# Three loads instead of five for the down weights of a decode step, with thirty-one unread products

## The chip, the cores and the metric

The kernel runs on one core of one Trainium2 chip. The metric is device time in microseconds (us), the median of repeated executions. One execution of each kernel was also taken with the hardware profiler; its span is some 2 us shorter than the time.

## The reference, cut to what matters

One token, model width 1024, passes an attention block with a large key and value cache and then a gated feed-forward layer of inner width 3584. The last step is what this study is about:

```python
h2 = h + (gelu(n @ w_gate) * (n @ w_up)) @ w_down     # n = layernorm(h); w_down is 3584 x 1024, bf16, 7.3 MB
```

All weights and caches, 173 MB, are read once.

## The kernel before

All loads go through one on-chip ring of 5 units of 16384 columns; SyncE issues them in program order and waits where a load overwrites data that is still to be read. The 28 "rows" of the down weights (128 x 1024 values each, 256 KB) come in five loads of falling size. Behind each load stand its products: per row four products of 128x256, one for each group of 32 output columns of the array, accumulating in the tile `f_ps`. Between them stand *unread products*: `keep_busy` multiplies data that is already there by an identity into a tile that nobody reads. They only give TensorE something to do while it would wait.

```python
def load(src, off=0):                       # next free place of the ring, one DMA
    ...
    nc.sync.dma_start(out=tv.rearrange("p (n w) -> p n w", w=w), in_=src)

# ... gate weights: one load; up weights: two loads of four rows, products into wu_ps, then
# transposes wu_t, the gate's product act_bf and its zero-padded form actz ...

wd_v = B_w_down.rearrange("(p c) n -> p c n", p=P)     # a load of n rows: n*2 KB in one run per partition
sizes = [14, 7, 4, 2, 1]
actz = padded(rows, act_bf[:], FC, "actz")
w_ps = row_bank("w_ps")

def keep_busy(n, src):
    for _ in range(n):
        mm(w_ps[:], ident_bf[:], src, True, True)      # 128x512, never read

keep_busy(8, wu[:, 0, 0:512])
busy = [3, 2, 1, 0, 0]
c0 = 0
for sz, nb in zip(sizes, busy):
    at[0] = 0
    wv = load(wd_v[:, c0:c0 + sz, :], c0 * D)
    for cc in range(sz):
        c = c0 + cc
        out_mm(actz[:, c, :], lambda g: wv[:, cc, g * OW:(g + 1) * OW], False, c + 1 == FC)   # 4 products
    c0 += sz
    keep_busy(nb, wv[:, 0, 0:512])
nc.vector.tensor_copy(out=o_fin[0:97, :], in_=f_ps[0:97, :])
nc.sync.dma_start(out=out[0, 0].rearrange("(g n) -> g n", n=OW), in_=o_fin[0:97:32, :])
```

## Time and profile before

| | before |
|---|---|
| time, median of 3 | 408.4 us (408.33 to 408.57) |
| span of the profiled run | 406.9 us |
| HBM reads | 173.02 MB at 425 GB/s |
| from the last up weights' landing to the last down weights' landing | 17.05 us |
| from the last landing to the end of the last product | 0.36 us |

The page of the profile, cut to four lines. The second and third have one digit for each fortieth of the span, in tenths: the clock granted to TensorE, and the busy share of the 16 DMA engines.

```profile
span 406.9 us, 2667 instructions
...
PEclk9986899987989999899996998999989899886889
DMA  9999999999999999999999999999999999999995
...
HBM read 173.02 MB, written 0.00 MB: 425 GB/s over the span
```

DMA is busy from the first slice to the last. Nothing that TensorE does counts unless it comes after the last landing or delays an issue. The end of the chain of waits (start, duration, what) says the same of the tail:

```profile
373.51 29.95 DMA ring<-in_B_w_down_dram
...
403.51 0.32 PE f_ps L145 x4
...
403.85 0.42 DVE o_fin L558
```

The timeline of TensorE's matmuls in the tail (start, duration, engine, line, operation, tiles, form, count; in brackets the idle time before and who ended it):

```profile
386.46 0.62 PE L145 MATMUL wu_ps<-ring,hnz 128*32 128x512 bf16 x4 [6.48 <-DMA ring<-in_B_w_up_dram]
...
391.47 1.89 PE L145 MATMUL w_ps<-ring,ident_bf 128*128 128x512 bf16 x8
395.00 1.71 PE L145 MATMUL f_ps<-ring,actz 128*32 128x256 bf16 x56 [1.63 <-DMA ring<-in_B_w_down_dram]
396.64 0.82 PE L145 MATMUL w_ps<-ring,ident_bf 128*128 128x512 bf16 x3
399.24 0.95 PE L145 MATMUL f_ps<-ring,actz 128*32 128x256 bf16 x28 [1.78 <-DMA ring<-in_B_w_down_dram]
400.12 0.61 PE L145 MATMUL w_ps<-ring,ident_bf 128*128 128x512 bf16 x2
401.67 0.62 PE L145 MATMUL f_ps<-ring,actz 128*32 128x256 bf16 x16 [0.94 <-DMA ring<-in_B_w_down_dram]
402.22 0.39 PE L145 MATMUL w_ps<-ring,ident_bf 128*128 128x512 bf16 x1
402.89 0.40 PE L145 MATMUL f_ps<-ring,actz 128*32 128x256 bf16 x8 [0.28 <-DMA ring<-in_B_w_down_dram]
403.51 0.29 PE L145 MATMUL f_ps<-ring,actz 128*32 128x256 bf16 x4 [0.21 <-DMA ring<-in_B_w_down_dram]
```

Each batch of `f_ps` products waits for its load: the starts at 395.00, 399.24, 401.67, 402.89 and 403.51 follow the landings by 0.04 to 0.05 us. TensorE has time to spare in every gap, and only the last four products lie behind the last landing.

### The profile page before, as it was taken

What the parts mean: (1) busy time and instruction counts of PE and PEld (TensorE: products, weight loads), DVE (VectorE), ACT (ScalarE), POOL (GpSimd) and SP (SyncE); (2) the same over time, 40 slices, a digit from 0 to 9 for tenths busy, and PEclk for the clock granted to TensorE, in tenths of its full rate; (3) what the DMA queues carried; (4) which work ended last, traced back from release to release, by engine and by line L of the source; (5) the groups of instructions that cost most, each with busy time, mean ns of one, the idle gap of its engine ahead of it and who ended that gap; (6) DMA issues with size and microseconds to landing.
All of it is one profiled execution on the core that took longest, in us unless ns stands there. A gap on an engine that the chain in (4) does not pass through costs nothing.

```text
span 406.9 us, 2667 instructions
## 1 busy us (share of the span) xinstructions
PE 293.1 (72%) x1495; PEld 60.8 (15%) x743; DVE 202.7 (50%) x185; ACT 44.7 (11%) x67; POOL 7.4 (2%) x17
## 2 busy tenths in 40 slices
PE   1346777769977699597776979976597969636283
PEld 0011111111111112111110111111111101212031
DVE  1118899955978359147971880879433000220110
ACT  1010000022000040100000420000041000100000
POOL 2000000000000000000000000000100000100000
PEclk9986899987989999899996998999989899886889
DMA  9999999999999999999999999999999999999995
GB/s 367 457 412 448 427 419 461 413 444 424 415 464 419 409 499 414 393 438 425 490 414 403 448 425 435 417 457 432 445 438 432 433 399 435 445 436 414 437 419 222
DMA packets 5213, 173.19 MB, mean 426 GB/s; under 512 B 585, under 2 KB 593, under 8 KB 849
## 3 DMA queue, kind: packets, MB, share of 16 engines
q1 hardware_dynamic: 5192, 173.02, 98.7%
q8 instruction: 9, 0.15, 0.1%
q14 instruction: 4, 0.02, 0.0%
q10 hardware_dynamic: 8, 0.00, 0.0%
HBM read 173.02 MB, written 0.00 MB: 425 GB/s over the span
## 4 chain that ended last, share of the span: by engine, by line
DMA 53%; PE 31%; DVE 12%; ACT 2%; issue 0%; SPq 0%; ACTq 0%
DMA ring<-in_A_v_cache_dram 31%; PE acc_ps L147 11%; DVE ring L281 9%; PE qk_ps L145 7%; DMA ring<-in_A_k_cache_dram 7%; DMA ring<-in_B_w_down_dram 7%; DMA ring<-in_B_w_gate_dram 7%; PE qk_ps L147 7%; PE acc_ps L145 4%; DVE mx L302 2%; ACT sc L301 2%; PE wg_ps L145 0%; PE wg_ps L147 0%; DVE pT L330 0%; ACT pe_r L327 0%
## 5 line engine op out<-in xcount | busy, mean ns | idle before, releaser
L281 DVE STREAM_TRANSPOSE ring<-ring 128x2048 uint32<-128x2048 uint32 x64 | 142.7, 2280 | 33.6 <-DMA ring<-in_A_k_cache_dram 33.5
L145 PE MATMUL qk_ps<-ring,wsel 128*128 128x512 bf16 x256 | 100.8, 394 | 35.8 <-DVE mx L302 23.6
L147 PE MATMUL acc_ps<-ring,pT 128*128 128x512 bf16 x384 | 114.1, 409 | 0.0
L147 PE MATMUL qk_ps<-ring,wsel 128*128 128x512 bf16 x256 | 100.6, 393 | 0.0
L145 PE MATMUL acc_ps<-ring,pT 128*128 128x512 bf16 x128 | 52.7, 412 | 20.4 <-DMA ring<-in_A_v_cache_dram 17.6
L145 PEld LDWEIGHTS <-wsel 128*128 128x128 bf16 x256 | 25.4, 99 | 135.1 <-issue 134.4
L301 ACT COPY sc<-qk_ps 128x1024 f32<-128x1024 f32 x16 | 16.2, 1011 | 176.8 <-PE qk_ps L147 176.7
L302 DVE TENSOR_REDUCE mx<-qk_ps 128x1 f32<-128x1024 f32 x16 | 19.6, 1222 | 26.0 <-ACT sc L301 26.0
L145 PEld LDWEIGHTS <-pT 128*128 128x128 bf16 x128 | 13.3, 104 | 119.1 <-issue 113.2
L357 DVE COPY acc_sb<-acc_ps 32x512 f32<-32x512 f32 x8 | 5.4, 672 | 36.6 <-PE acc_ps L147 36.6
L327 ACT ACTIVATE pe_r<-sc,nbias 128x1024 bf16<-128x1024 f32 x16 | 18.2, 1140 | 39.2 <-DVE nbias L322 38.5
L330 DVE STREAM_TRANSPOSE pT<-pe_r 128x1024 bf16<-128x1024 bf16 x16 | 19.0, 1226 | 6.2 <-ACT pe_r L327 6.2
L359 ACT COPY acc_sb<-acc_ps 32x512 f32<-32x512 f32 x8 | 4.6, 577 | 65.0 <-DVE acc_sb L357 65.0
L145 PE MATMUL q_ps<-ring,xnz 128*32 128x512 bf16 x32 | 5.2, 623 | 7.9 <-DMA ring<-in_A_wq_dram 7.9
L145 PE MATMUL wu_ps<-ring,hnz 128*32 128x512 bf16 x32 | 4.7, 503 | 7.8 <-DMA ring<-in_B_w_up_dram 7.8
L145 PE MATMUL wg_ps<-ring,hnz 128*32 128x512 bf16 x32 | 4.6, 517 | 7.7 <-DMA ring<-in_B_w_gate_dram 7.7
L145 PE MATMUL ln_tot<-ln_s,ones_f 128*128 128x1 f32 x8 | 1.9, 312 | 10.8 <-DVE ln_s L199 9.0
L315 DVE TENSOR_REDUCE gm<-mxT_ps 1x8 f32<-1x128 f32 x4 | 1.1, 279 | 16.1 <-PE mxT_ps L156 16.1
L145 PE MATMUL o_ps<-sel,acc_sb 128*128 128x8 f32 x32 | 4.2, 257 | 6.5 <-DVE rl L371 5.7
L145 PE MATMUL f_ps<-ring,actz 128*32 128x256 bf16 x112 | 4.0, 274 | 4.8 <-DMA ring<-in_B_w_down_dram 4.8
L237 DVE COPY q_ev<-q_ps 128x512 f32<-128x512 f32 x1 | 0.7, 692 | 13.3 <-PE q_ps L147 13.3
L237 DVE COPY wg_ev<-wg_ps 128x512 f32<-128x512 f32 x1 | 0.7, 691 | 11.6 <-PE wg_ps L145 11.6
(103 smaller groups left out, 89.2 us busy)
## 6 DMA issues: line engine op xcount, KB each, us to landing
ring<-in_A_k_cache_dram SPq DMA_DIRECT2D x16, 4096.0 KB, 33.9
ring<-in_A_wq_dram SPq DMA_DIRECT2D x2, 4096.0 KB, 16.5
ring<-in_A_wo_dram SPq DMA_DIRECT2D x2, 4096.0 KB, 30.8
ring<-in_B_w_gate_dram SPq DMA_DIRECT2D x1, 7168.0 KB
ring<-in_B_w_up_dram SPq DMA_DIRECT2D x2, 3584.0 KB, 30.5
ring<-in_B_w_down_dram SPq DMA_DIRECT2D x1, 3584.0 KB, 37.1
ring<-in_B_w_down_dram SPq DMA_DIRECT2D x1, 1792.0 KB
ring<-in_B_w_down_dram SPq DMA_DIRECT2D x1, 1024.0 KB, 29.3
```

The source lines that it names most:

```text
L145: return pe(t.matmul(out, lhsT=lhsT, rhs=rhs, start=start, stop=stop, tile_position=tile_position, skip_group_check=skip_group_check))
L147: op = t.add_instruction(mybir.InstMatmult(name=nc.get_next_instruction_name(), engine=t.engine, start_tensor_calc=start, stop_tensor_calc ...
L237: nc.vector.tensor_copy(out=dst, in_=src)
L281: dv(nc.vector.transpose(out=kt[:, c * w:(c + 1) * w], in_=kt[:, c * w:(c + 1) * w]))
L301: ac(nc.scalar.copy(out=sc[:], in_=flat))
L302: dv(nc.vector.tensor_reduce(out=state[("mx", g)][:, li:li + 1], in_=flat, axis=AX.X, op=ALU.max))
L315: dv(nc.vector.tensor_reduce(out=gm[:], in_=mxT_ps[:].rearrange("o (x h) -> o h x", h=rep), axis=AX.X, op=ALU.max))
L327: ac(nc.scalar.activation(out=pe_r[:], in_=state.pop(("sc", g, li))[:], func=ACT.Exp, bias=nbias[:, 0:1], scale=scale, accum_out=lpart[:, ...
L330: dv(nc.vector.transpose(out=pT[:].rearrange("p m c -> p (m c)"), in_=pe_r[:]))
L357: dv(nc.vector.tensor_copy(out=acc_sb[sl, :], in_=acc[sl, c, :]))
L359: ac(nc.scalar.copy(out=acc_sb[sl, :], in_=acc[sl, c, :]))
```

## The change

The intent is fewer loads without losing TensorE's clock. A first load of 22 rows lands late, and TensorE would wait so long for it that its clock is halved; thirty unread products are to bridge that.

```diff
-    sizes = [14, 7, 4, 2, 1]
+    sizes = [22, 5, 1]
...
-    keep_busy(8, wu[:, 0, 0:512])
-    busy = [3, 2, 1, 0, 0]
+    keep_busy(30, wu[:, 0, 0:512])
+    busy = [1, 0, 0]
```

Twenty-two rows are 22528 columns, more than a ring unit, so the first load now overwrites part of the gate weights and has to wait until they are read.

## The prediction

> **What bounds it now.** DMA. The page's slices show the DMA engines about nine tenths busy or more until the last of the 40 slices, 426 GB/s on average, 425 GB/s of HBM reads over a span of 406.9 us. At the end the chain of waits runs from the issue of the last down-weight load (373.5) through 29.95 us of DMA to its landing (403.46), then 0.3 us of products, a 0.42 us cast and the output's DMA. By the waits, the five loads (14, 7, 4, 2, 1 rows) let TensorE go on at 395.00, 399.24, 401.67, 402.89 and 403.51; the up weights did at 386.46. These 8.54, 4.24, 2.43, 1.22 and 0.62 us are 0.610, 0.606, 0.608, 0.61 and 0.62 us per row. A straight line through the largest and the smallest leaves about 0.01 us for a load itself. So a load costs nothing visible beyond its bytes, and removing two gives back at most 0.05 us.
>
> **What moves.** The bytes are the same. (1) Two DMAs go. (2) The first load now reaches into gate-weight space and is issued about 371.5 instead of 357.8 (views of SyncE); what is queued then lasts until 386.46, so the queue keeps 15 us of work: free. (3) TensorE works in 88 + 20 + 4 down products of four-at-a-time groups instead of 56 + 28 + 16 + 8 + 4, and in 30 + 1 unread products instead of 8 + 3 + 2 + 1.
>
> **Sums for the tail (estimates from the trace's durations).** Eight unread products took 1.89 us, 0.216 us apart, so thirty run from 391.47 to about 398.1. 22 rows should land at 386.46 + 22 x 0.609 = 399.85: TensorE idles 1.7 us. The old gaps of 1.63 and 1.78 us were followed by a granted clock of 1.00 (windows view); the gap of 6.48 us before the up weights was followed by 0.50. The Trainium skill, "TensorE: Matmul & The Clock Gate", Part 1, says that the clock is halved after an idle window of about 3.4 us; both observations agree, and 1.7 us should not trip it.
> 56 products took 1.64 us to the next instruction, 28 took 0.88: 27 ns each plus 0.12. So 88 take 2.5 us, until 402.4; one unread product brings 402.6; 5 rows land at 402.89, 20 products end their issue at about 403.5, just when the last row lands (403.5). The final four then follow as before, late by 0 to 0.1 us. The work moved into the tail just fits behind the DMA.
>
> **Net.** -0.05 to +0.1 us of 408.4: predicted 408.4 us, 407.8 to 409.0 eight times in ten. Chances: faster by over 2% 0.01, within 2% 0.98, slower by over 2% 0.01.
>
> **What the profile would show.** Last landing still about 17.05 us after the last up weights'; first down product at 399.8 or so after an idle time of about 1.7 us, at clock 1.00; no idle time, or under 0.4 us, before the second and third load's products; the last four starting within 0.1 us of the landing; cast and output as before.
>
> **What would make it wrong.** A half clock at 399.85: 88 products would then take some 4.9 us and the second and third batches follow late, +2 to +3 us, 410.5 to 411.5, still within 2%. The thirty starting at half clock (0.43 us each) would run past the landing; they have only 1.7 us of slack. A load's fixed cost hidden by the other loads in flight would make it faster by some tenths. Uneven DMA engines at the end (the DMA share falls from 1.0 at 401 to 0.6 at 402 while the last bytes land at 403) could shift the last landing by some tenths either way.

## The result, and the profile after

The changed kernel took 408.67 us in the median of 6 executions (408.40 to 408.83), the kernel before, in the same rounds, 408.49 us (408.33 to 408.91). The ratio is 1.0002 with a 95% interval of 0.9989 to 1.0015: the same. A ratio here and below is the mean time of one kernel's runs over that of the other's of the same rounds, so not quite the ratio of the medians.

The page, the same lines:

```profile
span 406.4 us, 2698 instructions
...
PEclk9965899998998899699998996989998989885979
DMA  9999999999999999999999999999999999999994
```

The end of the chain:

```profile
372.67 29.56 DMA ring<-in_B_w_down_dram
...
402.28 0.92 PE f_ps L145 x24
...
403.22 0.42 DVE o_fin L558
```

The timeline of the tail's matmuls:

```profile
385.96 0.62 PE L145 MATMUL wu_ps<-ring,hnz 128*32 128x512 bf16 x4 [6.52 <-DMA ring<-in_B_w_up_dram]
...
391.37 6.64 PE L145 MATMUL w_ps<-ring,ident_bf 128*128 128x512 bf16 x30
399.24 2.59 PE L145 MATMUL f_ps<-ring,actz 128*32 128x256 bf16 x88 [1.23 <-DMA ring<-in_B_w_down_dram]
401.75 0.39 PE L145 MATMUL w_ps<-ring,ident_bf 128*128 128x512 bf16 x1
402.28 0.89 PE L145 MATMUL f_ps<-ring,actz 128*32 128x256 bf16 x24
```

The last row's four products no longer have a line of their own: 20 + 4 products stand in one run, started by the landing of the 5 rows at 402.24. The chain ends there for the same reason, so it must not be read as "the last load no longer matters". The trace's landing events put the last row's landing at 402.83; 402.28 plus about 0.12 plus 20 times 27 ns is 402.9, and in the trace's records the last four products start at 402.88, just behind that landing. They end 0.36 us after it, as before the change. The two sides meet within 0.1 us.

The span is 0.5 us shorter than in the profile before, but 0.49 us of that came before the tail: the last up weights landed at 385.92 instead of 386.41, with no change made there. Profiles must therefore be compared from that landing on. In the table "tail" is the time from the last up weights' landing to the last down weights' landing, both from the trace's landing events (the last of each load's 16 completions); "after it" is from there to the end of the last product, by the chain.

| kernel | loads | tail, us | after it, us | sum |
|---|---|---|---|---|
| before | 14, 7, 4, 2, 1 | 17.05 | 0.36 | 17.41 |
| the change | 22, 5, 1 | 16.91 | 0.36 | 17.27 |

The tail got 0.14 us shorter in these two profiles. The times of one kernel spread over 0.3 to 0.7 us, so the times cannot show that.

### The profile page after: what moved, and what is told of

The parts are those of the page before. It is cut to its first block, busy times and chain, and to the rows that moved or that the text cites. A ratio compares the mean times of both kernels' runs of the same rounds, so it can differ in the third digit from the quotient of the medians.

```text
span 406.4 us, 2698 instructions
## 1 busy us (share of the span) xinstructions
PE 297.0 (73%) x1512; PEld 63.0 (16%) x760; DVE 202.6 (50%) x185; ACT 44.8 (11%) x67; POOL 7.4 (2%) x17
## 4 chain that ended last, share of the span: by engine, by line
DMA 53%; PE 30%; DVE 13%; ACT 2%; issue 1%; SPq 0%; ACTq 0%
DMA ring<-in_A_v_cache_dram 31%; PE acc_ps L147 12%; DVE ring L281 10%; DMA ring<-in_A_k_cache_dram 7%; DMA ring<-in_B_w_down_dram 7%; DMA ring<-in_B_w_gate_dram 7%; PE qk_ps L145 7%; PE qk_ps L147 6%; PE acc_ps L145 4%; DVE mx L302 2%; ACT sc L301 2%; PE wg_ps L145 0%; PE wg_ps L147 0%; DVE pT L330 0%; ACT pe_r L327 0%
## 5 line engine op out<-in xcount | busy, mean ns | idle before, releaser
L145 PE MATMUL w_ps<-ring,ident_bf 128*128 128x512 bf16 x31 | 7.0, 379 | 0.0
L145 PEld LDWEIGHTS <-hnz 128*32 128x32 bf16 x64 | 3.4, 119 | 19.7 <-issue 17.1
```

What stands on the lines that cost most here:

```text
L145: return pe(t.matmul(out, lhsT=lhsT, rhs=rhs, start=start, stop=stop, tile_position=tile_position, skip_group_check=skip_group_check))
```

## The experiments

All are edits of the changed kernel, and each was timed against the kernel before in the same rounds (whose medians were 408.49 to 408.65 us). The theory to be tested, **A**: only the last landing and what TensorE does after it count; the unread products pay for the late first load by keeping the clock; a load costs next to nothing itself. Rivals: the unread products do nothing; TensorE's issue is the bound at the end; or loads do cost something, and the saving was lost again in TensorE's work.

| label | loads | unread first | tail, us | after it, us | time, us (all executions) | ratio to before (95%) |
|---|---|---|---|---|---|---|
| a1_change_again | 22, 5, 1 | 30 | 16.92 | 0.36 | 408.59 (408.51 to 408.79) | 1.0003 (0.9990 to 1.0016) |
| e1_few_unread | 22, 5, 1 | 8 | 16.92 | 1.60 | 410.37 (409.94 to 410.93) | 1.0041 (1.0026 to 1.0056) |
| e2_old_loads_thirty | 14, 7, 4, 2, 1 | 30 | 16.98 | 0.36 | 408.58 (408.24 to 408.76) | 0.9995 (0.9981 to 1.0010) |
| e3_one_load | 28 | 50 | 16.91 | 3.31 | 411.74 (411.38 to 411.85) | 1.0071 (1.0055 to 1.0088) |
| e4_28_loads | 28 of one row | 8 | 17.95 | 0.47 | 409.81 (409.49 to 410.42) | 1.0028 (1.0013 to 1.0043) |
| e5_24_3_1 | 24, 3, 1 | 34 | 16.92 | 1.32 | 409.64 (409.26 to 409.77) | 1.0026 (1.0013 to 1.0039) |
| e7_small_packets | 22, 5, 1 | 30 | 17.84 | 0.36 | 410.65 (409.60 to 410.76) | 1.0047 (1.0034 to 1.0060) |
| e9_small_packets_36 | 22, 5, 1 | 36 | 17.84 | 0.36 | 409.47 (409.22 to 409.73) | 1.0020 (1.0006 to 1.0035) |
| e8_twenty | 22, 5, 1 | 20 | 16.94 | 0.36 | 409.96 (408.81 to 411.21) | 1.0039 (1.0023 to 1.0056) |
| e10_twentyfive | 22, 5, 1 | 25 | 16.91 | 1.69 | 410.11 (408.51 to 410.20) | 1.0031 (1.0020 to 1.0043) |

### The change once more

No edit.

> The change as it is, for a narrower interval on the same chip as the other runs of this call. Theory A (last landing bound, TensorE's work hidden): ratio to before 0.9990 to 1.0010; last landing 16.8 to 17.0 us after the up weights', last product ending 0.35 to 0.4 us after it.

Held on every point. Eleven executions of the change now lie between 408.40 and 408.83 us.

### The big load without its unread products

```diff
-    keep_busy(30, wu[:, 0, 0:512])
+    keep_busy(8, wu[:, 0, 0:512])
```

> Three loads as in the change (22, 5, 1 rows) but only 8 unread products before the first landing, as before the change. Theory A (the thirty are what pays for the big first load, through the clock): TensorE idles about 6.4 us, longer than the 3.4 us of a clock window, the first down products run at a granted clock of 0.50, about 53 ns each instead of 27, so the last product ends 2 to 3 us later against the last landing than the 0.36 us of the change; time +2.0 to +3.0 us, ratio to before 1.005 to 1.0075. Rival (the unread products do nothing): idle 6.4 us, clock 1.00, ratio within 0.001 of 1.

The timeline of the tail:

```profile
391.01 1.89 PE L145 MATMUL w_ps<-ring,ident_bf 128*128 128x512 bf16 x8
399.44 4.07 PE L145 MATMUL f_ps<-ring,actz 128*32 128x256 bf16 x88 [6.54 <-DMA ring<-in_B_w_down_dram]
...
403.76 0.84 PE L145 MATMUL f_ps<-ring,actz 128*32 128x256 bf16 x24
```

The 88 products took 4.07 us instead of 2.59, and the last product ended 1.60 us after the last landing. The rival falls: the thirty are needed. On average the expected size, +2 to +3 us, was too large; the ratio is worth 1.7 us. In the profiled execution the clock came back part of the way through the 88 products. It was one of two at 409.94 us; the other two took 410.80 and 410.93 us and were not profiled. The windows view of this run, cut along the steps at which the clock changed (stretch and its length; busy us and count of matmuls, of weight loads, of VectorE, ScalarE and GpSimd; granted clock; DMA share; GB/s), shows more:

```profile
392.29:395.70 3.41, 0.61 (x3) 0.19 (x2) 0.00 (x0) 0.00 (x0) 0.00 (x0) 1.00 1.01 436
395.70:399.12 3.42, 0.00 (x0) 0.00 (x0) 0.00 (x0) 0.00 (x0) 0.00 (x0) 0.50 0.72 307
399.12:402.53 3.41, 3.09 (x60) 2.61 (x63) 0.00 (x0) 0.00 (x0) 0.00 (x0) 0.50 0.72 298
```

The clock came back at 402.53. In all the profiles it moves only at the ends of such steps of 3.41 us. And it fell at 395.70, after a step in which TensorE had been busy for 0.61 us: a step need not be wholly idle. This was followed up below.

### The old loads with the thirty in front

```diff
-    sizes = [22, 5, 1]
+    sizes = [14, 7, 4, 2, 1]
...
-    busy = [1, 0, 0]
+    busy = [3, 2, 1, 0, 0]
```

> Five loads as before the change, with thirty unread products before the first. Theory A (everything but the last landing is hidden): the thirty end about 3 us after the first 14 rows landed, the down products catch up with the landings before the last row, whose four products start within 0.1 us of its landing; ratio 0.999 to 1.001. Rival (TensorE's issue is the bound at the end, so products ahead of landed data cost what they take): +3 us, ratio 1.007.

Theory A held. The first 14 rows had landed at 394.74 (landing events), their products began 3.2 us later, and nothing was lost:

```profile
391.34 6.64 PE L145 MATMUL w_ps<-ring,ident_bf 128*128 128x512 bf16 x30
397.91 1.71 PE L145 MATMUL f_ps<-ring,actz 128*32 128x256 bf16 x56
...
403.30 0.29 PE L145 MATMUL f_ps<-ring,actz 128*32 128x256 bf16 x4 [0.22 <-DMA ring<-in_B_w_down_dram]
```

From 397.91 until the last row the products ran without a wait (a line without a bracket has none, and that holds for the lines left out as well), behind their data; they caught up before the last row landed at 403.26. Work ahead of the last landing is free as long as TensorE can catch up; the rival, +3 us, falls.

### One load

```diff
-    sizes = [22, 5, 1]
+    sizes = [28]
...
-    keep_busy(30, wu[:, 0, 0:512])
-    busy = [1, 0, 0]
+    keep_busy(50, wu[:, 0, 0:512])
+    busy = [0]
```

> One load of 28 rows, fifty unread products to keep the clock. Theory A (only products that come after the last landing count, 27 ns each, and a load costs about 0.01 us itself): last landing 17.0 +/- 0.15 us after the last up weights' landing, then 112 products at clock 1.00 end about 3.4 us after it instead of 0.36: +3.0 us, ratio 1.0065 to 1.008. Rival B (each load costs about 0.07 us, which the change saved in silence and its tail gave back): last landing at 16.77 us, ratio 1.0060 to 1.0068. Rival C (products after the landing do not count): ratio 1.

All 112 products now stand behind the last landing, at full clock (the end of the chain):

```profile
372.92 30.14 DMA ring<-in_B_w_down_dram
...
403.10 3.27 PE f_ps L145 x112
```

They end 3.31 us after the landing, and the time rose by 0.71%, 2.9 us. So the products do cost their 27 ns each once they are behind the landing, and rival C falls. The tail, 16.91 us, is within the theory's range and 0.14 us from rival B's figure; with profiles that differ by up to 0.07 us for the same loads that is a weak decision, and the two experiments on the cost of a load make a better one.

### Is there room left in the split?

```diff
-    sizes = [22, 5, 1]
+    sizes = [24, 3, 1]
...
-    keep_busy(30, wu[:, 0, 0:512])
+    keep_busy(34, wu[:, 0, 0:512])
```

> Loads of 24, 3 and 1 rows, 34 unread products. Asks whether the split 22, 5, 1 has room left. Theory A: none; 24 rows land about 14.5 us after the up weights, their 96 products take 2.7 us, one unread product 0.2 us, the last 16 products 0.7 us: the last product ends about 18.1 us after the up weights' landing, 1.2 us after the last landing instead of 0.36, time +0.9 us, ratio to before 1.0015 to 1.003. Rival (there is room, the bound stays the last landing): last product 0.36 us after it, ratio as for the change.

Not two rows' worth. The end of the chain:

```profile
400.75 2.81 PE f_ps L145 x96
403.56 0.25 issue
403.81 0.65 PE f_ps L145 x16
```

The chain goes through the 96 products, without a landing between them and the end; they finish 1.32 us after the last landing, and the time rose by 0.26%, 1.1 us. Twenty-four rows in the first load are too many; 23 were not tried.

### The cost of a load: 28 loads

```diff
-    sizes = [22, 5, 1]
+    sizes = [1] * 28
...
-    keep_busy(30, wu[:, 0, 0:512])
-    busy = [1, 0, 0]
+    keep_busy(8, wu[:, 0, 0:512])
+    busy = [0] * 28
```

> Twenty-eight loads of one row, eight unread products. A magnifier for the cost of a load itself. Theory A (about 0.01 us a load): last landing 17.0 to 17.3 us after the last up weights' landing, ratio to before 0.9995 to 1.001. Rival B (0.07 us a load, as the two profiles' 17.06 us with five loads against 16.91 with three would have it): last landing at about 18.6 us, +1.6 us, ratio 1.004. Something else again if the issue of so many loads falls behind: then the issues on SyncE come later than the landings of the up weights and the DMA share drops before the end.

Neither figure came: the tail is 17.95 us, 0.90 more than with five loads, so 0.04 us a load. The DMA engines stayed full (busy shares of 1.03 to 1.06 from 386 to 402), so the issue did not fall behind. But twenty-eight loads also move much smaller pieces: a load moves one packet for each partition, of 2 KB here and of 44 KB for 22 rows. The next experiment separates the two.

The run showed something else as well. From 395 on TensorE had four products for every landing and never waited longer than 0.39 us, and yet the clock fell to 0.50 at 397.75. Four products with the array at full clock took 0.29 us, at half clock 0.40 (timeline):

```profile
397.23 0.29 PE L145 MATMUL f_ps<-ring,actz 128*32 128x256 bf16 x4 [0.35 <-DMA ring<-in_B_w_down_dram]
397.91 0.40 PE L145 MATMUL f_ps<-ring,actz 128*32 128x256 bf16 x4 [0.39 <-DMA ring<-in_B_w_down_dram]
```

### The cost of a load or of its packets

The rows are taken in another order, so that a load of n rows has n separate pieces of 2 KB for each partition.

```diff
-    wd_v = B_w_down.rearrange("(p c) n -> p c n", p=P)
+    wd_v = B_w_down.rearrange("(c p) n -> p c n", p=P)
```

> Wrong result on purpose: the down weights read in another row order, so that each load of the change (22, 5, 1 rows, thirty unread products) moves packets of 2 KB in place of one packet of up to 44 KB a partition; still three loads. Asks what made 28 loads 0.9 us slower to land. If packets (smaller ones, 28 a partition in both): last landing 17.7 to 18.0 us after the up weights', ratio 1.0015 to 1.0030. If the load itself (its completion, 28 against 3): 16.8 to 17.0 us, ratio 0.999 to 1.001.

The tail is 17.84 us against 16.92 with large packets. The packets from 386 to 405 us (DMA view), first in this run:

```profile
DMA packets 3431, 6.96 MB, mean 366 GB/s; under 512 B 48, under 2 KB 48, under 8 KB 3429
```

and in the change once more:

```profile
DMA packets 411, 6.34 MB, mean 334 GB/s; under 512 B 48, under 2 KB 48, under 8 KB 176
```

The edit changed the order of the rows along with the packets, but the packet records in the traces speak against the order: a packet of 2 KB took 84 ns in this run, 85 with the 28 loads, and 84 also in the last load of the kernel before and of the change, where the order is the old one. One of 44 KB took 1670 ns, 76 for each 2 KB. The records of 2 KB packets overlap a little (1.05 in flight for each engine on average, against 1.00 with large ones), so a small packet costs about 84 / 1.05 - 76 = 4 ns more than the same bytes in a large one (an estimate). The engines had work all the time, although the third load was issued only at 390.0 us, behind an issue of the second that took 16.9 us.

So the packets cost 0.92 us, and what 28 loads add over three at the same packet size is 0.11 us (17.95 less 17.84), about 0.004 us a load, from one profile of each. An estimate from the 0.92 us, which agrees with the records: each of 16 engines moved 25 packets more for each of its 8 partitions, 200 in all, 0.0046 us each. Going from five loads to three saves 16 packets an engine, 0.07 us; the profiles show 0.04 to 0.14 (17.05 and 16.98 us with five loads, 16.91 to 16.94 with three). Rival B was right that fewer loads shorten the tail, but neither in the price of a load nor in the reason.

The time, however, rose by 1.9 us, twice as much as the tail. The profiled execution was the fastest of the four (409.60 us, the others 410.62 to 410.76), so the profile does not show what the others lost. The guess was the clock, since the 22 rows landed later and TensorE idled longer. The same kernel with more unread products tests it:

```diff
-    keep_busy(30, wu[:, 0, 0:512])
+    keep_busy(36, wu[:, 0, 0:512])
```

> The small packets again (wrong result on purpose), with 36 unread products in place of 30. The run with 30 landed 0.92 us later but took 1.9 us more in three executions of four. If the rest was the clock (the later landing left an idle time of up to 2.2 us, long enough for a window with a matmul share below 0.4): the four executions now agree, at the last landing's +0.9 us alone, ratio to before 1.0015 to 1.0030. Rival (small packets cost the program another 1 us that the one profile did not show): ratio 1.004 to 1.006 again.

The four executions now lie between 409.22 and 409.73 us, and the ratio, 1.0020, is worth 0.8 us, the tail's share alone. That six more unread products removed the second microsecond is shown; that it was the clock is inferred, as no profile caught a slow execution of the first version.

### When is the clock halved?

The Trainium skill, "TensorE: Matmul & The Clock Gate", Part 1, gives half clock as the state "after ≥1 idle window (~3.4µs)", in windows that run freely. The prediction took from this that an idle time of 1.7 us is safe. The lines of the first experiment and of the 28 loads said otherwise, so the profiles were cut into steps of 3.413 us along their clock records. The matmul share is the time in which a matmul was running, over 3.413 us. Over all twelve profiles:

| matmul share of a step at full clock | steps followed by half clock | by full clock |
|---|---|---|
| below 0.39 | 137 | 0 |
| 0.39 to 0.50 | 19 | 37 |
| 0.50 to 0.65 | 16 | 146 |
| over 0.65 | 1 | 715 |

No step had to be idle. The cut at 0.39 was laid just below the lowest share that kept full clock here (0.395); it describes these steps and is not a measured threshold. Two runs test this on the changed kernel, with fewer unread products:

```diff
-    keep_busy(30, wu[:, 0, 0:512])
+    keep_busy(20, wu[:, 0, 0:512])
```

> The change with 20 unread products in place of 30: TensorE idles about 3.9 us before the first landing. Theory 1 (the clock is halved only after a wholly idle window of 3.4 us): at most one execution in six is touched, ratio to before 1.000 to 1.0008. Theory 2 (it is halved after a window in which the share of matmul time is below about 0.4, as the windows of all profiles so far show, with no such window followed by full clock): nearly every execution has one such window, the down products run at 0.50, time +1.0 to +1.8 us, ratio 1.002 to 1.0045.

```diff
-    keep_busy(30, wu[:, 0, 0:512])
+    keep_busy(25, wu[:, 0, 0:512])
```

> The change with 25 unread products: idle time of about 2.7 us. Theory 2 (half clock after a window of 3.41 us with a matmul share below 0.4, that is over 2.05 us of idle time in it; windows run freely): (3.41 + 2.7 - 4.1) / 3.41, about six executions in ten are touched, between 409.4 and 411.3 us, the others like the change; ratio 1.001 to 1.003. Theory 1 (only a wholly idle window of 3.4 us): none touched, ratio 0.999 to 1.001.

With 20, five of six executions took 409.54 to 411.21 us and one 408.81; with 25, five of six took 409.98 to 410.20 and one 408.51. Theory 1 expected at most one in six, and none. Theory 2 expected nearly all and about six in ten; five of six is within what chance allows for both. With 20 the profile fell on the one execution that was spared, with 25 on one that was not; for the other slow executions the half clock is inferred from their times. Their steps, with 20 first:

```profile
394.27:397.69 3.42, 1.71 (x8) 0.68 (x7) 0.00 (x0) 0.00 (x0) 0.00 (x0) 1.00 0.94 407
397.69:401.10 3.41, 1.48 (x56) 1.48 (x59) 0.00 (x0) 0.00 (x0) 0.00 (x0) 1.00 0.79 334
```

```profile
393.71:397.13 3.42, 3.01 (x14) 1.27 (x13) 0.00 (x0) 0.00 (x0) 0.00 (x0) 1.00 1.07 464
397.13:400.54 3.41, 1.12 (x43) 1.12 (x46) 0.00 (x0) 0.00 (x0) 0.00 (x0) 1.00 0.83 349
400.54:403.95 3.41, 3.41 (x61) 2.37 (x53) 0.00 (x0) 0.00 (x0) 0.00 (x0) 0.50 0.36 141
```

With 20 an idle time of 3.64 us, longer than a step, fell across two steps: shares of 0.50 (1.71 / 3.42) and 0.43, and the clock stayed. With 25 an idle time of 2.70 us, shorter than a step, left one step with a share of 0.33, and the clock fell. So the idle time alone does not decide; where it lies in the steps does, in these two profiles, and that is chance.

The change's steps across its idle time: 397.96 to 401.37, busy for 2.18 of 3.41 us, a share of 0.64:

```profile
397.96:401.37 3.41, 2.18 (x81) 2.20 (x84) 0.00 (x0) 0.00 (x0) 0.00 (x0) 1.00 0.86 363
```

## Why the prediction was right

- **The bound.** Right. DMA is the bound to the last landing, and what follows it is 0.36 us of products before and after. That work ahead of the last landing is free was tested by delaying it 3 us (no change in time) and by putting it behind the landing (+2.9 us for 112 products at once).
- **"So a load costs nothing visible beyond its bytes, and removing two gives back at most 0.05 us."** The sign was right and the size too small. The tail was 16.91 to 16.94 us with three loads and 16.98 to 17.05 with five, 0.04 to 0.14 us, about 0.1. The step that misled is the straight line: it was put through the waits' ends, and a wait ends with the last of a load's 16 engines. In the landing events that engine's lag behind the first one shrank from 2.00 to 1.91 us over the five loads, which hid the price. By each load's first completion, the loads of 7, 4, 2 and 1 rows came 4.26, 2.46, 1.24 and 0.64 us after the load before; a line through these has 0.604 us a row and 0.036 us a load. That is what 8 packets for each engine, which every load has whatever its size, cost by the estimate above (8 x 0.0046 us); beyond its packets a load costs about 0.004 us. The prediction had named "a load's fixed cost hidden by the other loads in flight" among its risks.
- **The late issue is free.** Right: SyncE issued the first load at 370.97 instead of 357.83, and the busy share of the DMA engines stayed at 0.97 from 357 to 371, 1.03 from 371 to 386 and 0.99 from 386 to 397 (windows view).
- **TensorE's sums.** Right. 88 products to the next instruction took 401.75 - 399.24 = 2.51 us (predicted 2.5), the thirty 6.64 us, the last four products met their landing within 0.1 us.
- **The first landing and the idle time.** Predicted 399.85 after 1.7 us, measured 399.24 after 1.23. Of the 0.6 us, 0.49 is that all of the tail came earlier in this execution; the rest is the shorter tail. The second profile of the change had 1.62 us.
- **The clock.** The outcome was right (1.00 throughout the tail), the reason only in part. That 1.7 us is half of 3.4 did not make it safe: by the table above every step seen fell to half clock once it was idle for more than 61%, 2.08 us (3.41 x 0.61), and 35 of 218 fell with a matmul share of 0.39 to 0.65, the band in which 1.7 us of idle time within one step lies (0.50). All eleven executions of the change stayed at 408.83 us or below, so it held here; the prediction's better ground was the old gaps of 1.63 and 1.78 us in the same place, and for the rest it was lucky. Twenty-five unread products instead of thirty, 2.70 us of idle time, were too few.
- **The risk.** "+2 to +3 us" for half clock was too large on average: +1.7 us with 8 unread products, where the profiled execution shows the clock coming back after one busy step (matmul share 0.91), within the 88 products. It was not too large for every execution: with 8 they took 1.3 to 2.3 us more, and two with 20 took 411.2 us, 2.7 more; none of these slower ones was profiled.

Where the small gain went: 0.14 us by the two profiles is below the spread of 0.3 to 0.7 us between executions of one kernel. No run here resolves it in the time, and it is not claimed as a gain.

No version tried beats both kernels. What is left in the tail was seen but not tried: the 16 completions of one load are spread over 1.7 to 2.4 us, in every profile, and the last one counts.

## What to carry to other kernels

When DMA is the bound, sort the work into what lies before the last landing and what lies behind it: the first is free as long as the engine catches up, the second costs its full duration, so the last load should be small and the one before it just as large as the engine can work off while the last ones land. Fewer, larger loads then bring only what their fewer, larger packets save (here 0.1 us of 408, seen in the profiles and not in the times). Unread products that hold the clock should leave far less idle time than one of the 3.41 us steps in which the clock moves (1.23 and 1.62 us held here, 2.70 did not), because what counts is the busy share of a step, and how the idle time falls across the steps is chance.

## What the Trainium skill lacked or had wrong

- "TensorE: Matmul & The Clock Gate", Part 1, names an idle window of about 3.4 us as what halves the clock. The step length agrees (3.413 us, with another phase in each run), but the window need not be idle: all 137 full-clock steps with a matmul share below 0.39 were followed by half clock, the lowest share kept at full clock was 0.395, and 19 of 56 steps between 0.39 and 0.50 fell as well. In the run with 28 loads the clock fell while TensorE never waited longer than 0.39 us. The page does report, under "A second HAM failure mode", a kernel whose clock swings because short idle times come often enough, but it gives no share. Nor does the matmul share alone settle it between 0.39 and 0.65; what else does was not studied.
- The same page asks for one busy window to get the full clock back, without saying how busy. In the twelve profiles no step with a matmul share below 0.76 (102 of them) brought it back, and 142 of 143 with a share over 0.88 did.
- "DMA: Bandwidth & Descriptors", Specifications, gives 512 B as the transfer from which a DMA runs at line rate. With packets of 2 KB the 22 rows (22 x 262144 B) took 13.97 us to land, 413 GB/s; with packets of 44 KB 13.27 us, 435 GB/s. Its section "Why small descriptors are slow (HBM only)" gives a fixed cost of 3 cycles for each packet, worked out for 256 B; here 2 KB still cost 5%. Worked out in the same way for 2 KB (an estimate: 3 cycles on 2048 / 32 = 64) the section's figure is 4.7%, which agrees; so it is the 512 B that these runs do not bear out.
- "DMA: Bandwidth & Descriptors", "Why a DMA increments its semaphore by 16 and not by 1", says that the engines finish independently. The traces agree, and add how far apart: 1.7 to 2.4 us between the first and the last engine of one load of the down weights, for small and large loads alike, with one queue in use. The page has no figure for it.
